# Attention scores as products 64 rows deep, with the queries as they were loaded

## The chip, the core and the metric

The kernel runs on one core of one Trainium2 chip. The time is what the device takes for one execution, in microseconds (us). The engines named are TensorE (PE, with its weight loads PEld), VectorE (DVE), ScalarE (ACT), GpSimd (POOL) and SyncE (SP), which here issues loads and stores.

## What is computed

Attention in eight heads over eight sequences of 576 tokens, then a mixture of eight experts with a capacity, greedily assigned. Cut to what matters:

```python
q, k, v: (8, 8, 576, 64) float32        # batch, head, token, depth
scores = q @ k.T / 8
rel = pos[:, None] - pos[None, :]
mask_plain = (rel >= 0) & (rel < 32)                    # heads 0 to 3
mask_dil = (rel >= 0) & (rel < 128) & (rel % 4 == 0)    # heads 4 to 7
attn = softmax(where(mask, scores, -1e9))
x = attn @ v                            # (4608, 512) after merging heads
logits = x @ w_gate                     # (4608, 8)
# the pairs (token, expert) in order of falling logit, each token to one expert, 576 tokens to each
for e in range(8):
    out[mask_e] = relu(x[mask_e] @ w1[e]) @ w2[e]
```

## The kernel before

The program has two parts, attention and the experts, with the router between them. In each part a small planner (`Schedule`, line 154) takes operations with an engine, an estimated cost, their dependencies, a due time and, for products, a pool of PSUM tiles; it runs through them in planned time and writes every engine's instructions down in the order that it finds. On the chip each engine then works through its own list in that order.

**Units.** Attention goes through 32 units, four a batch: two of plain heads, two of dilated ones, each for two heads (the two halves `a`). The depth is 64, so two heads stand above each other in the 128 partitions. A plain unit has 9 blocks of 64 queries against 96 keys; a dilated one, after sorting the tokens by residue, 12 blocks of 48 queries against 80 keys.

**Queries.** `load` (line 340) brings the queries of a batch into a staging tile `QS` and copies them from there into `QT` (lines 362 to 367), where each block has 2 x 64 columns (the dilated 2 x 48 of 128) and each head only its own half of the rows, with zeros in the other half, put there once by `zero` (line 311). A product over all 128 rows against these columns gives both heads' scores beside each other. The copies are spread over GpSimd, VectorE and ScalarE (`Q_ENG`). Queries, keys and values have two buffers, by the parity of the batch.

**One unit** (`build`, line 420):

- `scan` (line 482): bf16 products of the upper halves of the float32 words, 128 rows by 128 columns of queries against the block's keys; `most` (line 487) finds each row's masked maximum with VectorE; one product (line 436) turns the maxima, and a VectorE copy puts them into `R` (line 440).
- `scores` (line 495), in three groups of 3 (plain) or 4 (dilated) blocks: a bf16 selector product (line 501) adds mask and maximum for each block, then the float32 product of keys and queries (line 504) adds the scores. A float32 product stands in the trace as two records, each with a weight load. The weights are the block's keys (96 or 80 columns), and the queries are streamed.
- an exponential on ScalarE for each group (line 454), from PSUM into `E`.
- `values` (line 506): for each block and head a product with `V` into 64 partitions of a tile; `weigh` (line 514) divides by the sums.

**After the units** (`banks`, line 543): results are transposed (line 562) and kept in `xt` by ScalarE. After the last unit of a batch come the router's logits: four products whose weights are the padded gate weights `wgp`, one in each quarter of the columns, over 288 tokens (line 588), a copy into `L4` (line 596), a transpose for each 128 tokens (line 607), and a VectorE sum over the four quarters into `Lt` (line 613). `choose` then makes keys for the router, and `coarse` and `coarse_counts` (lines 707 and 712) count them into columns of the PSUM tile `pz`, chunk by chunk, with a low due time.

**PSUM** has eight banks: two for `scan`, two for `scores`, three (`PV`) shared by values, transposes and logits, and one, `pz`, for the router. Until the kernel is warm one of the three is used for idle products that keep the clock up.

SP's list holds the loads and stores in order; a load of keys waits for the scores of two batches before, since those read the same buffer.

Of the kernel before, what the change touches and what calls it, by code (L numbers as in the profile page):

```python
# [30 lines left out]
NK = 16  # L31
# [104 lines left out]
class Buf:  # L136
    def __init__(self, pool):
        self.pool, self.users, self.tile = pool, [], None
# [15 lines left out]
class Schedule:  # L154
# [18 lines left out]
    def place(self, x):  # L173

        best = None
        for i, h in enumerate(x.buf.pool.held):
            if h and any(u.end is None for u in h.users):
# [63 lines left out]
def attention(tc, ctx, C, load_const, T, xd, Lt, R):  # L241
# [8 lines left out]
    def ring(pool, shape, dtype, name, n):  # L250
# [7 lines left out]
    QS = [ring(pk, [128, 2, S] if x == 0 else [128, 8, SR], F32, f"qs{x}", 1) for x in range(2)]  # L258
# [6 lines left out]
    L4 = ring(pk, [128, 2 * S], F32, "L4", 1)  # L265
    PRE = ring(pk, [128, 256], BF, "pre", 2)
    wgp = pk.tile([128, 4, 32], F32, name="wgp")
# [4 lines left out]
    def qv(kind, s):  # L272
        t = QT[kind][s]
        if kind == 0:
            return t.rearrange("p (u c a i) -> p u c a i", u=2, c=NB, a=2)
        return t.rearrange("p (h c a i) -> p h c a i", h=8, c=3, a=2)
# [34 lines left out]
    def zero(kind, s, part, eng):  # L311

        jx = slice(part, part + 1) if kind == 0 else slice(4 * part, 4 * part + 4)
        t = qv(kind, s)[:, jx]
        e = nc.vector if eng == "DVE" else nc.gpsimd

        def fn():
            e.memset(t[64:, :, :, 0], 0.0)
            e.memset(t[:64, :, :, 1], 0.0)
            if kind == 1:  # L320
                for a in range(2):
                    e.memset(t[64 * a:64 * a + 64, :, :, a, QB[1]:], 0.0)

        ready["z", kind, s, part] = op(eng, 1200 if eng == "DVE" else 1000 if kind == 0 else 1700, fn)

# [14 lines left out]
    def load(b, kind, part=None):  # L340
# [7 lines left out]
        if not part:  # L348
            load.q = QS[kind].take()
            load.old = old("k", kind, s)  # L350
        qs, oldq, useq = load.q
        lq = sp(1, lambda: nc.sync.dma_start(qs[:, ix], q[b][:, ix]), oldq, nb, b)
        lk = sp(1, lambda: nc.sync.dma_start(KT[kind][s][:, ik], k[b][:, ik]), load.old, nb, b)
        dst = qv(kind, s)
        nq = QB[kind]
        oldd = old("q", kind, s) if not part else []
        for p in range(2) if part is None else (part,):
            cs = []
            for a in range(2):
                pr = slice(64 * a, 64 * a + 64)  # L360
                jx = slice(p, p + 1) if kind == 0 else slice(4 * p, 4 * p + 4)
                src = qs[pr, jx].rearrange("p u (c i) -> p u c i", i=nq)
                o = dst[pr, jx, :, a, :nq]
                eng = Q_ENG[kind][2 * p + a] if b else ("ACT", "DVE")[a]
                f = {"ACT": act, "DVE": nc.vector.tensor_copy, "POOL": nc.gpsimd.tensor_copy}[eng]
                cost = {"ACT": 670, "DVE": 370 if kind else 670, "POOL": 2050}[eng]
# [1042 lines left out]
```

## Time and profile before

| | us |
|---|---|
| median of 3 runs | 728.65 (728.17 to 731.08) |
| run of the profiled execution | 729.1 |
| its span | 727.3 |
| TensorE products, busy | 672.8 (93%) |
| weight loads, busy | 589.5 (81%) |
| VectorE, busy | 499.1 (69%) |
| ScalarE, busy | 280.5 (39%) |
| GpSimd, busy | 121.5 (17%) |

The page divides the span into 40 slices of 18.2 us; each digit is the busy share of a slice in tenths, PEclk the granted TensorE clock in tenths, and the last row what the DMA engines moved in GB/s.

```profile
PE   6979999999984799998799999999999999999994
PEclk9889999999995799999799999999999999999998
DMA  9999987874120620812612702621441474122001
GB/s 255 246 254 321 284 248 223 247 202 107 36 66 31 211 59 19 278 52 66 204 58 53 248 35 66 200 99 52 148 150 51 146 232 160 44 94 95 1 23 43
```

Attention takes the first twelve slices (to 212 us), the router's first search the thirteenth (to 240 us), and the rest is the experts. A record of a product lasts longer than the engine is held by it, since products are pipelined: what counts is the distance from one start to the next.

### The profile page before, as it was taken

Reading aid. Unit: us, or ns where it says so; the run is one execution under the profiler, and the core shown is the slowest. Engines: PE = TensorE matmul, PEld = TensorE weight load, DVE = VectorE, ACT = ScalarE, POOL = GpSimd, SP = SyncE. Lnnn points to the kernel's source line nnn. Section 1 sums busy time; section 2 is a strip of 40 time slices with the busy share of each in tenths; the row PEclk is TensorE's granted clock in tenths of the full one; section 3 lists DMA queues with packets and bytes.
Section 4 is the critical chain, followed back from the end, with each engine's and each line's share of the span. In section 5 each row is a group of like instructions: output and inputs, shape, how many; then the busy total and the mean of one; then the engine's idle time right before and its main releaser. Section 6 shows DMA issues by size and latency. Waiting matters only on the chain.

```text
span 727.3 us, 17284 instructions
## 1 busy us (share of the span) xinstructions
PE 672.8 (93%) x6554; PEld 589.5 (81%) x6555; DVE 499.1 (69%) x2109; ACT 280.5 (39%) x593; POOL 121.5 (17%) x180
## 2 busy tenths in 40 slices
PE   6979999999984799998799999999999999999994
PEld 4868899899964498797579979978978988988983
DVE  5546776878647798888769969968967973733300
ACT  2335545453430631542433623523533434434210
POOL 6111111000000300500310410321131041041011
PEclk9889999999995799999799999999999999999998
DMA  9999987874120620812612702621441474122001
GB/s 255 246 254 321 284 248 223 247 202 107 36 66 31 211 59 19 278 52 66 204 58 53 248 35 66 200 99 52 148 150 51 146 232 160 44 94 95 1 23 43
DMA packets 55067, 98.30 MB, mean 135 GB/s; under 512 B 5828, under 2 KB 27460, under 8 KB 54980
## 3 DMA queue, kind: packets, MB, share of 16 engines
q1 hardware_dynamic: 49096, 78.32, 36.6%
q0 software_dynamic: 5888, 18.88, 7.7%
q8 instruction: 51, 0.84, 0.5%
q14 instruction: 32, 0.26, 0.1%
HBM read 78.31 MB, written 18.87 MB: 134 GB/s over the span
## 4 chain that ended last, share of the span: by engine, by line
PE 56%; DVE 15%; issue 13%; DMA 11%; POOL 2%; ACT 1%; SPq 1%; POOLq 0%; DVEq 0%; ACTq 0%
PE py L1275 14%; PE ph L1233 13%; PE pS L504 7%; PE px L512 5%; DMA xg<-xd,idx 3%; DMA qs<-in_qd 3%; DMA qs<-in_qp 3%; PE px L562 2%; DVE hb L1253 2%; PE pS L501 2%; PE ptx L1196 2%; DVE G L734 2%; PE pm L484 2%; PE py L1278 2%; PE py L1280 2%
## 5 line engine op out<-in xcount | busy, mean ns | idle before, releaser
L1275 PE MATMUL py<-w2h,hb 128*128 128x512 f32 x512 | 172.6, 402 | 0.0
L1233 PE MATMUL ph<-xh,w1h 128*128 128x256 f32 (+1 forms) x512 | 138.7, 301 | 0.5 <-ACT xh L1078 0.5
L1233 PE MATMUL ph<-xl,w1h 128*128 128x256 f32 (+1 forms) x512 | 136.3, 297 | 0.0
L1233 PE MATMUL ph<-xh,w1l 128*128 128x256 f32 (+1 forms) x512 | 136.3, 297 | 0.0
L1275 PEld LDWEIGHTS py<-w2h,hb 128*128 128x128 f32 x512 | 97.3, 190 | 19.8
L1078 ACT ACTIVATE hb<-ph 128x256 fp32r<-128x256 f32 (+2 forms) x192 | 59.7, 346 | 117.5 <-PE ph L1233 117.0
L1275 PE MATMUL py<-w2l,hb 128*128 128x512 f32 x256 | 101.0, 394 | 1.0 <-DVE w2l L1079 1.0
L1233 PEld LDWEIGHTS ph<-xh,w1h 128*128 128x128 f32 x512 | 91.8, 189 | 1.2 <-ACT xh L1078 0.6
L1233 PEld LDWEIGHTS ph<-xl,w1h 128*128 128x128 f32 x512 | 91.5, 189 | 0.0
L1233 PEld LDWEIGHTS ph<-xh,w1l 128*128 128x128 f32 x512 | 91.5, 189 | 0.0
L504 PE MATMUL pS<-q,k 128*80 128x96 f32 (+1 forms) x672 | 84.5, 268 | 0.0
L1301 POOL DMA_INDIRECT out<-y,idx x40 | 41.5, 1038 | 223.4 <-ACT y L1078 157.4
L1253 DVE SCALAR_TENSOR_TENSOR hb<-ph,hb 128x256 fp32r<-128x256 f32 (+1 forms) x128 | 57.0, 452 | 24.6 <-ACT hb L1078 24.2
L454 ACT ACTIVATE E<-pS 96x384 f32<-96x384 f32 (+1 forms) x96 | 46.1, 486 | 67.3 <-PE pS L504 58.4
L504 PEld LDWEIGHTS pS<-q,k 128*80 128x80 f32 (+1 forms) x672 | 70.0, 161 | 0.0
L1078 ACT ACTIVATE y<-py 128x512 f32<-128x512 f32 (+1 forms) x40 | 23.9, 596 | 110.5 <-PE py L1275 98.5
L491 DVE CUSTOM_DVE_ANT_0 junkm<-pm,const 128x80 bf16<-128x80 f32 (+1 forms) x336 | 59.7, 243 | 8.9 <-PE pm L484 8.5
L1275 PEld LDWEIGHTS py<-w2l,hb 128*128 128x128 f32 x256 | 48.8, 191 | 10.2 <-DVE w2l L1079 1.5
L1079 DVE TENSOR_TENSOR w2l<-raw,w2h 128x512 fp32r<-128x512 f32 x64 | 42.1, 684 | 19.4 <-ACT w2h L1078 19.2
L1078 ACT ACTIVATE w1h<-raw 128x512 fp32r<-128x512 f32 x64 | 39.7, 630 | 35.8 <-DMA raw<-in_moe_w 35.3
L512 PE MATMUL px<-v,E 81*64 81x65 f32 (+1 forms) x1344 | 48.5, 227 | 4.3 <-DMA v<-in_vp 1.8
L1183 POOL DMA_INDIRECT xg<-xd,idx x40 | 43.3, 1082 | 45.0 <-issue 30.3
(160 smaller groups left out, 993.6 us busy)
## 6 DMA issues: line engine op xcount, KB each, us to landing
raw<-in_moe_w SPq DMA_DIRECT2D x128, 256.0 KB, 4.5
v<-in_vp SPq DMA_DIRECT2D x8, 780.0 KB, 9.9
v<-in_vd SPq DMA_DIRECT2D x8, 650.0 KB, 9.5
xd<-xs SPq DMA_DIRECT2D x16, 288.0 KB, 8.8
xd<-xs SPq DMA_DIRECT2D x32, 144.0 KB, 8.6
qs<-in_qp SPq DMA_DIRECT2D x7, 576.0 KB, 9.3
k<-in_kp SPq DMA_DIRECT2D x7, 576.0 KB, 4.0
k<-in_kd SPq DMA_DIRECT2D x7, 576.0 KB, 5.7
```

The costliest lines, as they stand in the source:

```text
L454: e = self.op("ACT", 380, lambda j=j, pS=pS: nc.scalar.activation(self.E[:self.nk, j * self.gs:j * self.gs + self.gs], pS.tile[:, :self.gs ...
L484: nc.tensor.matmul(pm[:, (c - c0) * self.nk:(c - c0 + 1) * self.nk], self.Qh[c], self.Kh[c], start=True, stop=True)
L491: nc.vector.tensor_tensor_reduce(out=jk[:, c - c0, :nk], in0=pm[:, (c - c0) * nk:(c - c0 + 1) * nk], in1=mm[:, min(1, (c if self.kind == 0 ...
L504: nc.tensor.matmul(pS[:nk, c - c0], self.Ks[c], self.Qm[c], start=False, stop=True, skip_group_check=True)
L512: nc.tensor.matmul(px[64 * a:64 * a + 64, c - c0], lh, self.V[c][a], start=True, stop=True)
L1078: act = lambda o, i, f=AF.Copy: nc.scalar.activation(o, i, f)
L1079: sub = lambda e, o, a, b: e.tensor_tensor(o, a, b, op=OP.subtract)
L1183: nc.gpsimd.indirect_dma_start(out=xg[:n], out_offset=None, in_=xd, in_offset=bass.IndirectOffsetOnAxis(ap=box[0][:n, m:m + 1], axis=0))
L1233: nc.tensor.matmul(o, a[:, d * 128:d * 128 + 128], b[:, d, c0:c1], start=((d, i) == pairs[0]), stop=((d, i) == pairs[-1]))
L1253: hl = op("DVE", 335 if j == 0 else 400, lambda: nc.vector.scalar_tensor_tensor(hb[:, CAP + c0:CAP + c1], o, 0.0, hb[:, c0:c1], op0=OP.max ...
L1275: nc.tensor.matmul(py, x, w, start=(f + i == 0), stop=(f == NF - 1 and i == 2))
L1301: s = nc.gpsimd.indirect_dma_start(out=out, out_offset=bass.IndirectOffsetOnAxis(ap=box[0][:n, m:m + 1], axis=0), in_=y[:n], in_offset=None)
```

## The change

Queries are loaded straight into `QT`; the staging tiles, the copies and the zeroed halves are gone. A block's scores are two products, one for each head, each over that head's 64 rows; the two heads' results lie in different banks of a PSUM tile that has two. The selector product is split in the same way, though it keeps its 73 or 76 rows. `scan` too has two products a block, from 64 rows into 64 partitions each. The exponential reads both banks and writes `E` in the order of before.

The logits have tokens in partitions: `xt` is the weight (128 tokens), and the gate weights are streamed (8 columns), four products a chunk of 128 tokens that add up in PSUM; a batch of 576 tokens has four whole chunks and a half one. Two VectorE copies bring them into `Lt`. The transposes of line 607 and the tile `L4` are gone.

PSUM: two banks for `scan`, two tiles of two banks for `scores` and now the transposes of line 562 too, and for values and logits one bank and `pz`. Since `pz` is in use until then, the router's coarse counts are all made after the last unit, from flags kept for all chunks; the flags are made as before. `Buf` can now ask for one certain tile of its pool.

The planner's costs change with it (in ns).

```diff
+C_S = 620
-Q_ENG = (("POOL", "POOL", "POOL", "ACT"), ("DVE", "DVE", "ACT", "ACT"))
...
-    QT = [[pk.tile([128, 2 * NB * 128] if x == 0 else [128, 8 * 3 * 128], F32, name=f"q{x}{s}") for s in range(2)]
+    QT = [[pk.tile([128, 2 * S] if x == 0 else [128, 8 * SR + 16], F32, name=f"q{x}{s}") for s in range(2)]
...
-    PM, PS, PV = (Pool([ps.tile([128, 512], F32, name=f"{n}{i}") for i in range(k)])
-                  for n, k in (("pm", 2), ("pS", 2), ("px", 3)))
+    PM = Pool([ps.tile([128, 512], F32, name=f"pm{i}") for i in range(2)])
+    PS = Pool([ps.tile([128, 2, 512], F32, name=f"pS{i}") for i in range(2)])
+    PV = Pool([ps.tile([128, 512], F32, name="px0"), R.pz])
...
+        n = (S, SR)[kind]
+        dst = QT[kind][s][:, :2 * S].rearrange("p (u n) -> p u n", n=n)
+        lq = sp(1, lambda: nc.sync.dma_start(dst[:, ix], q[b][:, ix]), load.old[0], nb, b)
+        lk = sp(1, lambda: nc.sync.dma_start(KT[kind][s][:, ik], k[b][:, ik]), load.old[1], nb, b)
         for p in range(2) if part is None else (part,):
...
+            ready["q", kind, b, p] = [lq, lk]
...
-            self.Qm = [Q[:, x, c, :, :nq] for x, c in L]
-            self.Ks = [K_[:, x, k0[c]:k0[c] + nk] for x, c in L]
+            two = [slice(0, 64), slice(64, 128)]
+            self.Qm = [[Q[p, x * nq0 + nq * c:x * nq0 + nq * c + nq] for p in two] for x, c in L]
+            self.Ks = [[K_[p, x, k0[c]:k0[c] + nk] for p in two] for x, c in L]
...
-                a = self.op("PE", 42 * (c1 - c0), lambda c0=c0, c1=c1, pm=pm: self.scan(c0, c1, pm.tile), qk, B_A, pm)
+                a = self.op("PE", 40 + 50 * (c1 - c0), lambda c0=c0, c1=c1, pm=pm: self.scan(c0, c1, pm.tile),
+                            [*qk, ready["pad"]] if kind else qk, B_A, pm)
...
-                d = self.op("DVE", (177 if kind == 0 else 162) * (c1 - c0),
+                d = self.op("DVE", (290 if kind == 0 else 270) * (c1 - c0),
...
-                c = self.op("PE", 850, lambda j=j, pS=pS: self.scores(j, pS.tile), [rc, *qk, ready["c", 1 + kind]], 0, pS)
+                c = self.op("PE", C_S, lambda j=j, pS=pS: self.scores(j, pS.tile), [rc, *qk, ready["c", 1 + kind]], 0, pS)
...
             for c in range(c0, c1):
-                nc.tensor.matmul(pm[:, (c - c0) * self.nk:(c - c0 + 1) * self.nk], self.Qh[c], self.Kh[c],
-                                 start=True, stop=True)
+                for a in range(2):
+                    nc.tensor.matmul(pm[64 * a:64 * a + 64, (c - c0) * nk:(c - c0 + 1) * nk], self.Qh[c][a], self.Kh[c][a],
+                                     start=True, stop=True)
...
+            o = lambda c, a: pS[:nk, a, (c - c0) * nq:(c - c0 + 1) * nq]
             for c in range(c0, c0 + gs):
+                for a in range(2):
+                    nc.tensor.matmul(o(c, a), ls[:64 + n, c], self.r[:64 + n, a * nq:a * nq + nq], start=(c == c0), stop=False,
+                                     skip_group_check=True)
             for c in range(c0, c0 + gs):
+                for a in range(2):
+                    nc.tensor.matmul(o(c, a), self.Ks[c][a], self.Qm[c][a], start=False, stop=True, skip_group_check=True)
...
+        def logits():
+            for c, p, n in h + parts:
+                o = pt.tile[p:p + n, NE * (c - c0):NE * (c - c0) + NE]
                 for g in range(4):
+                    t0 = 128 * c + p - b * S
+                    nc.tensor.matmul(o, xt_[b, g // 2][0][:, g % 2, t0:t0 + n], wg[:, g], start=(g == 0), stop=(g == 3))
```

More of the change, by code (lines that the diff above doesn't have):

```diff
@@ L136, with __init__ @@
 class Buf:
-    def __init__(self, pool):
-        self.pool, self.users, self.tile = pool, [], None
+    def __init__(self, pool, only=None):
+        self.pool, self.users, self.tile, self.only = pool, [], None, only
 class Ring:
@@ L176, in place @@
         for i, h in enumerate(x.buf.pool.held):
-            if h and any(u.end is None for u in h.users):
+            if h and any(u.end is None for u in h.users) or x.buf.only not in (None, i):
                 continue
@@ L309, in attention @@
     ready = {}
[L311 to L324, printed above, removed]
     def frame(kind):
@@ L348, in load @@
         if not part:
[L349 to L356, printed above, removed]
-        for p in range(2) if part is None else (part,):
[L358 to L366, printed above, removed]
-                c = op(eng, cost, lambda o=o, src=src, f=f: f(o, src), [lq, ready["z", kind, s, p], *oldd], -4 * b * P_U)
-                useq.append(c)
-                cs.append(c)
-            ready["q", kind, b, p] = [*cs, lk]
+            load.old = old("q", kind, s), old("k", kind, s)
+        n = (S, SR)[kind]
+        dst = QT[kind][s][:, :2 * S].rearrange("p (u n) -> p u n", n=n)
+        lq = sp(1, lambda: nc.sync.dma_start(dst[:, ix], q[b][:, ix]), load.old[0], nb, b)
+        lk = sp(1, lambda: nc.sync.dma_start(KT[kind][s][:, ik], k[b][:, ik]), load.old[1], nb, b)
+        for p in range(2) if part is None else (part,):
+            ready["q", kind, b, p] = [lq, lk]
     def load_values(b, kind):
@@ new lines, in banks, with settle @@
+        t = un.op("PE", 2000, logits, [*xt_[b], ready["w"]], B_K, pt)
+        for kk in range(2):
+            xt_[b, kk][2].append(t)
+        def settle():
+            for c, p, n in h:
+                nc.vector.tensor_copy(Lt[p:p + n, c], pt.tile[p:p + n, NE * (c - c0):NE * (c - c0) + NE])
+            ca = parts[0][0]
+            nc.vector.tensor_copy(Lt[:, ca:c1], pt.tile[:, NE * (ca - c0):NE * (c1 - c0)].rearrange("p (c e) -> p c e", e=NE))
+        x = un.op("DVE", 340, settle, [t], B_K)
@@ L631, in attention @@
-    fill, warm = PV.tiles[2], R.zero
-    PV.held[2] = Buf(PV)
+            f = op("DVE", 196, lambda c=c: R.coarse(c, PRE[:, c]), [x], late)
+            if c == 0:
+                counts.append([])
+            counts[0].append((c, f))
+        if b < B - 1:
+            return
+        hold = Buf(PV, 1)
+        hold.users.append(Op(-1, "PE", 0, None, (), 0, 0, 0, None))
+        prev = None
+        for c, f in counts[0]:
+            prev = op("PE", 60, lambda c=c: R.coarse_counts(c, PRE[:, c]), [f, ready["c", 3], prev, un.last], late,
+                      buf=None if prev else hold)
@@ L633, in attention @@
+    counts = []
+    fill, warm = PS.tiles[1][:, 0], R.zero
+    PS.held[1] = Buf(PS)
     keep_clock(nc, warm, fill, F0)
@@ L641, in idle, with pad @@
                 keep_clock(nc, warm, fill, int(max(0, gap - 400) / 430))
-    zero(0, 0, 0, "DVE")
-    zero(0, 0, 1, "POOL")
-    for kind, s in ((1, 0), (0, 1), (1, 1)):
-        for part in range(2):
-            zero(kind, s, part, "POOL")
-    op("DVE", 300, lambda: nc.vector.memset(R.pz[:, :256], 0.0), (), B_P)
+    def pad():
+        for s in range(2):
+            nc.gpsimd.memset(QT[1][s][:, 8 * SR:], 0.0)
+    ready["pad"] = op("POOL", 200, pad)
     for part in range(2):
@@ L812, in search_alone @@
             nc.vector.tensor_scalar(flag[:w, 1:], ps, float(CAP), None, op0=OP.is_ge, op1=OP.max, accum_out=flag[:w, :1])
+            if it == 2 and not last:
+                nc.vector.memset(self.pz[:, :256].rearrange("p (c k) -> p c k", k=32)[:, :, NK:], 0.0)
             nc.tensor.matmul(self.pa[:, :1 + NE], C[f"unit{it}"][:w], flag[:w], start=True, stop=True)
```

92 lines of the change are left out of this document (23 added, 69 removed).

## The prediction

> **What bounds the kernel now.** I read the stretches of 20 us first (columns: length; busy us and count of TensorE products, of its weight loads, of VectorE, ScalarE and GpSimd; granted clock; DMA share; GB/s), then TensorE's waits in the first 212 us.
>
> ```profile
> 0.00:20.00 20.00, 13.96 (x126) 10.23 (x127) 11.26 (x74) 5.71 (x10) 11.78 (x30) 0.91 0.91 261
> 20.00:40.00 20.00, 17.33 (x277) 16.05 (x274) 10.53 (x76) 5.54 (x11) 2.18 (x4) 0.91 1.05 241
> 40.00:60.00 20.00, 15.72 (x232) 14.34 (x233) 7.78 (x60) 9.05 (x17) 1.99 (x3) 0.83 1.01 273
> ...
> 120.00:140.00 20.00, 20.00 (x348) 17.95 (x347) 14.19 (x91) 9.44 (x18) 1.99 (x3) 1.00 0.69 214
> ...
> 180.00:200.00 20.00, 20.00 (x327) 18.32 (x327) 13.93 (x96) 8.58 (x17) 0.00 (x0) 1.00 0.14 32
> ```
> ```profile
> PE pm L484 <- DVE q L367: 6.0, 2, 5.3
> PE px L512 <- DMA v<-in_vp: 1.8, 1, 1.8
> PE px L512 <- DMA v<-in_vd: 1.6, 1, 1.6
> PE pm L436 <- DVE mx L491: 1.5, 2, 1.1
> ```
>
> Attention lasts until about 212 us of the span. Up to 60 us the DMA engines are full, TensorE now and then waits (the four largest waits: 10.9 us together), and its clock is granted at 0.91, 0.91 and 0.83, which is 7 us of full clock lost. From 100 us on the DMA share falls and TensorE has no pause: 20.00 of 20. A busy TensorE is a modelled figure, so I checked it in the timeline of its products (start, length with overlap, count):
>
> ```profile
> 98.65 0.33 PE L501 MATMUL pS<-R,const 73*96 73x128 bf16 x3
> 98.82 0.85 PE L504 MATMUL pS<-q,k 128*96 128x128 f32 x6
> 99.50 0.33 PE L501 MATMUL pS<-R,const 73*96 73x128 bf16 x3
> 99.67 0.85 PE L504 MATMUL pS<-q,k 128*96 128x128 f32 x6
> 100.36 0.33 PE L501 MATMUL pS<-R,const 73*96 73x128 bf16 x3
> 100.53 0.85 PE L504 MATMUL pS<-q,k 128*96 128x128 f32 x6
> 101.31 1.28 PE L512 MATMUL px<-v,E 97*64 97x65 f32 x36
> 102.51 0.22 PE L436 MATMUL pm<-const,mx 128*12 128x128 bf16 x1
> 102.66 0.87 PE L562 MATMUL px<-const,xs 128*128 128x128 f32 x6
> 103.37 0.38 PE L484 MATMUL pm<-k,q 128*128 128x96 bf16 x5
> 103.59 0.33 PE L501 MATMUL pS<-R,const 76*80 76x96 bf16 x4
> 103.77 0.85 PE L504 MATMUL pS<-q,k 128*80 128x96 f32 x8
> 104.45 0.34 PE L484 MATMUL pm<-k,q 128*128 128x96 bf16 x4
> 104.63 0.33 PE L501 MATMUL pS<-R,const 76*80 76x96 bf16 x4
> 104.80 0.85 PE L504 MATMUL pS<-q,k 128*80 128x96 f32 x8
> 105.49 0.38 PE L484 MATMUL pm<-k,q 128*128 128x96 bf16 x5
> ```
>
> Each group starts when the one before has been fed. So what a piece costs is the distance from its start to the next start, and the change is worth what it does to these distances. A float32 product stands there as two records (three blocks, x6), each with a weight load of its own.
>
> **Three prices from these rows.** *Scores, one group.* Plain head: selector 98.65 to 98.82, 0.17; products 0.68; 0.85 in all. Dilated: 0.18 + 0.68 = 0.86.
>
> *Changing how the array is divided.* The last record of line 504 before the values starts at 101.10, so the values should follow 0.11 later; they start at 101.31. Line 436 streams 128 columns, which takes line 501 0.055 (three in 0.17); the next piece starts 0.15 after it, at 102.66. Both are about 0.095 us more than the streaming: the array empties between products that fill all columns and those that use 64 or 12. Between lines 504, 501, 562 and 484, all undivided, nothing is lost.
>
> ```profile
> 101.10 0.27 PE L504 MATMUL pS<-q,k 128*96 128x128 f32 x1
> ```
>
> *Weight loads.* The loads' groups by shape, 80 to 208 us (rows*columns; busy us, mean ns):
>
> ```profile
> L504 PEld LDWEIGHTS pS<-q,k 128*80 128x80 f32 x283 | 25.4, 150 | 0.0
> L504 PEld LDWEIGHTS pS<-q,k 128*96 128x96 f32 x180 | 20.5, 163 | 0.0
> L512 PEld LDWEIGHTS px<-v,E 97*64 97x64 f32 x360 | 11.4, 137 | 1.5
> ...
> L501 PEld LDWEIGHTS <-const 73*96 73x96 bf16 x90 | 7.9, 123 | 0.9 <-issue 0.7
> ...
> L436 PEld LDWEIGHTS <-mx 128*12 128x12 bf16 x10 | 0.8, 84 | 1.0 <-DVE mx L491 0.3 <-issue 0.2
> ```
>
> From 64 to 96 float32 columns the load grows by 26 ns, 0.81 ns a column; the rest is latency that overlaps. So 96 columns hold the load path for 78 ns, 80 for 65, 128 for 104. Where a load is not hidden one sees it: the first load of a group starts at 100.47, the second at 100.56, and with 80 columns at 103.72 and 103.79.
>
> ```profile
> 100.47 0.16 PEld L504 LDWEIGHTS pS<-q,k 128*96 128x96 f32 x1
> 100.56 0.17 PEld L504 LDWEIGHTS pS<-q,k 128*96 128x96 f32 x1
> 103.72 0.15 PEld L504 LDWEIGHTS pS<-q,k 128*80 128x80 f32 x1
> 103.79 0.23 PEld L504 LDWEIGHTS pS<-q,k 128*80 128x80 f32 x2
> ```
>
> I take 0.083, 0.069 and 0.110 us, swap included. In bf16, (123 - 84)/84 = 0.46 ns a column: 0.045 for 96, 0.037 for 80. Today every score load hides behind a stream as long or longer (128 or 96 columns, 0.109 or 0.083 us a record). That is what the change undoes: it halves the streams (64 or 48 columns) and leaves the loads at 96 and 80.
>
> **The change, part by part.**
>
> *Products.* Each block's product becomes two, 64 rows deep, one for each half. No row shows halves split by rows. By columns it is shown: 36 records of line 512 in 101.31 to 102.51 are 0.033 each, though each streams 65 columns in two steps (0.055), so two run at a time, their loads too. I take the same here: three blocks x two passes = 6 pairs, each as long as its load: 6 x 0.083 + the last stream 0.054 = 0.55; dilated 8 x 0.069 + 0.04 = 0.59. Ends: streams alone, 6 x 0.056 and 8 x 0.043, both 0.34; no overlap, 12 x 0.083 = 1.00 and 16 x 0.069 = 1.10.
>
> *Selector.* Twice the records with half the columns: 6 x 0.045 = 0.27 and 8 x 0.037 = 0.30, against 0.17 and 0.18 if the load stayed hidden.
>
> *Array emptied on the way in.* The selector is 73 or 76 rows deep, so it can't stand in a half: whole array, then halves. I take 0.095 from the column case; ends 0 and 0.15 (the distance with the load behind it). The group: 0.27 + 0.095 + 0.55 = 0.915 against 0.85; dilated 0.30 + 0.095 + 0.59 = 0.985 against 0.86. Sum 0.19 x 48 = **+9 us**.
>
> The Trainium skill, "TensorEngine Tiling (Array Packing)", "Key Properties", says that a change of tiling mode drains TensorE, and it lists 64-row tiles as a mode of their own; by that the 0.095 holds for rows too, and the trace agrees for columns alone. Its "TensorE: Matmul & The Clock Gate", "LDWEIGHTS", has the load go by columns and not by rows, so that 64 rows would shorten none; no row here shows a 64-row load.
>
> *On the way out.* The last group of a unit is followed by its values, where the division changes today already (100.53). The other groups above (98.82, 99.67, 103.77, 104.80) are followed by a piece where today nothing changes and then something would. Two of three, 64 of 96, each 0.095 + a bf16 load of 0.045 that no stream hides = 0.14: **+9 us**.
>
> *Scan* (line 484): from 128x128 to two 64x64 quarters a block, 45 ns as before if they overlap; each scan changes the division, about one new change per scan beyond those counted: 64 x 0.12 = **+8 us**. Ends 0 and 64 x 0.35 = 22 (quarters one after the other).
>
> *Logits.* Line 588 took 1.11 (113.17 to 114.28, below), the transposes of line 607 0.11 each, 4.5 a batch: 1.6 together. Now tokens are the weights: 4 chunks x 4 x 2 loads of 128 columns, and 8 of 64: 32 x 0.110 + 8 x 0.055 = 3.96, and the half chunk of 64 tokens divides the columns, 0.24. +2.6 x 8 = **+21 us**. If the loads cost half: 2.2, +5 us.
>
> ```profile
> 113.17 1.18 PE L588 MATMUL px<-xt,wgp 128*32 128x288 f32 x16
> 114.28 0.62 PE L484 MATMUL pm<-k,q 128*128 128x80 bf16 x12
> ```
>
> *Removed: query copies and zeroing.* No byte of DMA goes: as many loads, into the query tile itself, in SP's same order; a query load now waits for the scores two batches back instead of a copy, and behind it on SP stands the key load, which waits for the same scores today. The copies are off the path after 60 us: GpSimd waited on TensorE, not the reverse.
>
> ```profile
> POOL q L367 <- PE pS L504: 58.8, 6, 18.2
> ```
>
> So nothing there. Early they bring what TensorE waits: of 10.9 us of waits and 7 us of lost clock I take **-12 us**, which a longer TensorE covers in any case; ends -18 and 0.
>
> *PSUM.* Score groups and 7 transposes a batch share two slots, each held some 1.5 us (0.9 TensorE, 0.49 the exponential below, and latencies): 19 x 1.5 / 2 = 14 us of a batch. A batch is four units, and the unit above lasts from 98.65 to 103.59, 5 us, before its logits. Cost nothing, hidden by TensorE's other pieces; at most +5.
>
> ```profile
> L454 ACT ACTIVATE E<-pS 96x384 f32<-96x384 f32 (+1 forms) x96 | 46.1, 486 | 67.3 <-PE pS L504 58.4
> ```
>
> *Counts* (line 712) move behind the last unit, where TensorE waits for VectorE: nothing, at most +2. The planner's new costs put the same pieces in another order; with TensorE never short of work I take nothing, ends -3 and +3. VectorE loses copies and is not the bound (14 of 20).
>
> Sum: 9 + 9 + 8 + 21 - 12 = **+35 us**. The profiled span is 727.3, its run 729.1, the median of three 728.65; I add to the median: **763**. Router and experts, from 212 us, are as before.
>
> **Rivals.** *A. Row halves don't empty the array.* No row excludes it. Then 9 + 9 of the drains go (96 x 0.095 and the way out): +17, **745**.
>
> *B. Faster: the loads don't bind.* If a load in a half holds the path only half as long, products take 0.34, the selector 0.17, and the array isn't emptied for rows: -0.31 x 96 = -30, scan +8, logits +5: -17, of which the first 45 of 212 us, full of DMA, give little: -15, **714**. It decides from loads of about 0.7 of their length, where the sum of A before the covered waits (28 to -17) crosses zero. Against it stand 0.09 and 0.07 in the four load rows. The Trainium skill, "TensorEngine Tiling (Array Packing)", "Theoretical Speedup", promises up to 2x at 64 rows, which is this case.
>
> *C. The halves don't overlap* (the change doesn't do what it says): products +0.45 and +0.51 a group, 48 x 0.96 = +46 on top: **809**.
>
> *D. B's loads, but the array is emptied:* -17 + 18, about **729**.
>
> **Numbers.** Forecast 0.47, A 0.16, B 0.22, C 0.06, D 0.09. B and a quarter of D come out faster by over 0.5% (about what a measurement of this kernel tells from no change): 0.24; within it 0.06, most of D; slower 0.70, the rest. The range 710 to 785 takes in B, D, A and the forecast with its ends (clock and waits, PSUM); C is left out. The slower cases alone span 740 to 785.
>
> **What would show it.** Right: score pairs 0.083 apart (plain) and 0.069 (dilated), a gap of some 0.1 at lines 501 to 504 and back, logits near 4 us a batch, attention ending near 247 us. Wrong: pairs 0.055 apart (B), no gap (A), single products 0.083 apart (C). If TensorE pauses on ScalarE or VectorE after 100 us, the PSUM step is wrong.

## The result, and the profile after

The changed kernel takes 869.04 us (median of 4 runs, 855.38 to 882.97) against 729.69 (4 runs): a ratio of **1.180, interval 1.166 to 1.193**. The forecast of 763 and its whole range, to 785, were far too low. The ratio is that of the two shorter runs (855.38 and 866.04, mean granted clock 0.837 and 0.822); the profiled execution is one of the two longer, with a run of 872.05, a span of 870.3 and a clock of 0.816.

First the page's slices of the changed kernel's span (40, each 21.8 us, in tenths; PEclk is the granted clock):

```profile
PE   6999999999999999749999799999999999999995
...
PEclk7556555559688575559999799999999999999998
```

TensorE is busy at nine tenths and more in nearly every slice, and its clock is granted in half through most of the first sixteen. The stretches of attention say it in numbers (columns as in the prediction: length; busy us and count of TensorE products, weight loads, VectorE, ScalarE, GpSimd; granted clock; DMA share; GB/s). The changed kernel:

```profile
0.00:60.00 60.00, 51.97 (x679) 44.63 (x684) 21.77 (x180) 10.06 (x19) 0.59 (x10) 0.60 0.99 251
60.00:200.00 140.00, 139.89 (x1683) 125.91 (x1679) 49.66 (x364) 29.54 (x56) 0.00 (x0) 0.54 0.41 120
200.00:219.00 19.00, 19.00 (x382) 17.30 (x379) 10.16 (x71) 5.59 (x11) 0.00 (x0) 1.00 0.53 131
219.00:345.00 126.00, 125.09 (x1781) 113.51 (x1780) 45.11 (x298) 32.39 (x63) 0.00 (x0) 0.68 0.29 83
```

The kernel before:

```profile
60.00:212.00 152.00, 149.37 (x2490) 134.44 (x2487) 110.78 (x738) 73.29 (x141) 9.98 (x15) 1.00 0.70 195
```

The third number from the end is the one to read: before, the clock is whole from 60 us on; after, it is 0.54 and 0.68 in stretches in which TensorE has no pause (139.89 of 140, 125.09 of 126). Nor does it wait for another engine there; from 100 to 345 us the table of TensorE's waits has one row, 0.9 us:

```profile
PE pS L468 <- ACT xt L269: 0.9, 2, 0.4
```

The last batch's logits are the last large piece of attention (40 records from 348.73, 7.95 us at half clock). Behind them and the router's counts comes the first product of the router's search, of line 745 now and of line 788 before. In the timelines (start, length, count), after:

```profile
359.57 0.25 PE L745 MATMUL py<-flagc,const 128*128 128x1 bf16 x2 [0.27 <-DVE junkc L742]
```

Before:

```profile
217.05 0.25 PE L788 MATMUL py<-flagc,const 128*128 128x1 bf16 x2 [0.27 <-DVE junkc L785]
```

What follows took 727.3 - 217.1 = 510 before and 870.3 - 359.6 = 511 now, so **all of the loss, some 142 us, is in attention**.

The changed kernel has its full clock for twenty microseconds at a time, and there its pieces can be timed as the prediction did, from start to start. In the changed kernel line 468 is the selector, 472 the scores, 449 the scan, 398 the turn-product, 559 the logits. Its timeline of TensorE at full clock:

```profile
204.35 0.57 PE L449 MATMUL pm<-k,q 64*64 64x96 bf16 x18
204.88 0.44 PE L468 MATMUL pS<-R,const 73*96 73x64 bf16 x6
205.25 0.72 PE L472 MATMUL pS<-q,k 64*96 64x64 f32 x12
205.90 0.46 PE L468 MATMUL pS<-R,const 73*96 73x64 bf16 x6
206.28 0.72 PE L472 MATMUL pS<-q,k 64*96 64x64 f32 x12
206.94 0.22 PE L398 MATMUL pm<-const,mx 128*9 128x128 bf16 x1
...
209.64 0.48 PE L468 MATMUL pS<-R,const 76*80 76x48 bf16 x8
210.05 0.78 PE L472 MATMUL pS<-q,k 64*80 64x48 f32 x16
210.76 0.48 PE L468 MATMUL pS<-R,const 76*80 76x48 bf16 x8
```

A plain group is 1.02 and 1.04 (204.88, 205.90, 206.94), a dilated one 1.12; the scan of nine blocks is 0.53, where 45 ns a block before make 0.40. And a batch's 40 logits records at full clock:

```profile
215.37 4.30 PE L559 MATMUL pz<-wg,xt 128*64 128x8 f32 x40
```

The same group at half clock:

```profile
106.59 0.66 PE L468 MATMUL pS<-R,const 73*96 73x64 bf16 x6
107.18 1.23 PE L472 MATMUL pS<-q,k 64*96 64x64 f32 x12
108.34 0.27 PE L398 MATMUL pm<-const,mx 128*12 128x128 bf16 x1
```

That is 1.75, 1.7 times as long. So the loss can be added up. The added work at full clock is what the prediction summed: 9 + 9 + 8 + 21 = 47. The clock lost in attention, from the four rows, is 0.40 x 60 + 0.46 x 140 + 0.32 x 126 = 129 us of full clock, and 7 more from 345 us to the end at half clock. A piece that takes 1.7 at half clock and 1 at full loses 0.7/1.7 = 0.41 of its time, not half, so I estimate that 136 x 0.41/0.5 = 112 could be had back. The kernel before lost 7 us of full clock, or 6 in the same way. 47 + 112 - 6 = 153, against some 142 measured. The rest may be half clock that full DMA queues hid in the first 60 us, and early waits that went; the two largest, 6.0 and 1.8 us before, are now these:

```profile
PE pm L449 <- DMA k<-in_kp: 3.4, 2, 2.8
PE pS L468 <- ACT E L416: 2.3, 5, 0.6
```

**The work forecast is there, and twice as much again is clock.**

### The profile page after: what moved, and what is told of

It is laid out like the page before. It is cut to its first block, busy times and chain, and to the rows that moved or that the text cites. A ratio compares the mean times of both kernels' runs of the same rounds, so it can differ in the third digit from the quotient of the medians.

```text
span 870.3 us, 20086 instructions
## 1 busy us (share of the span) xinstructions
PE 824.2 (95%) x8056; PEld 728.3 (84%) x8060; DVE 485.4 (56%) x2074; ACT 266.5 (31%) x567; POOL 95.2 (11%) x138
## 3 DMA queue, kind: packets, MB, share of 16 engines
q8 instruction: 63, 1.03, 0.5%
## 4 chain that ended last, share of the span: by engine, by line
PE 71%; DVE 11%; issue 10%; DMA 3%; POOL 2%; ACT 1%; SPq 1%; POOLq 0%; DVEq 0%
PE py L1234 13%; PE ph L1192 12%; PE pS L472 11%; PE pS L468 6%; PE pS L530 4%; PE px L480 4%; PE px L559 4%; PE pz L480 4%; PE pm L449 3%; PE pz L559 2%; DMA xg<-xd,idx 2%; DVE hb L1212 2%; PE ptx L1155 2%; DVE G L691 1%; PE py L1237 1%
## 5 line engine op out<-in xcount | busy, mean ns | idle before, releaser
L472 PE MATMUL pS<-q,k 64*80 64x48 f32 (+1 forms) x1344 | 103.2, 312 | 0.0
L472 PEld LDWEIGHTS pS<-q,k 64*80 64x80 f32 (+1 forms) x1344 | 88.2, 219 | 4.8
L976 POOL TENSOR_TENSOR rx<-oa,const 128x360 bf16<-128x360 bf16 x8 | 7.5, 936 | 497.3 <-DVE oa L971 497.3
L468 PE MATMUL pS<-R,const 76*80 76x48 bf16 (+1 forms) x672 | 58.4, 235 | 3.5 <-ACT E L416 2.3
L468 PEld LDWEIGHTS <-const 76*80 76x80 bf16 (+1 forms) x672 | 49.6, 160 | 11.0 <-issue 3.4
L1234 PEld LDWEIGHTS py<-w2l,hb 128*128 128x128 f32 x256 | 48.8, 191 | 10.2 <-DVE w2l L1038 1.5
L269 ACT ACTIVATE xt<-pS 128x288 f32<-128x288 f32 (+1 forms) x56 | 32.2, 604 | 69.1 <-PE pS L530 67.5
```

Source lines behind the costliest of these rows:

```text
L468: nc.tensor.matmul(o(c, a), ls[:64 + n, c], self.r[:64 + n, a * nq:a * nq + nq], start=(c == c0), stop=False, skip_group_check=True)
L472: nc.tensor.matmul(o(c, a), self.Ks[c][a], self.Qm[c][a], start=False, stop=True, skip_group_check=True)
L1234: nc.tensor.matmul(py, x, w, start=(f + i == 0), stop=(f == NF - 1 and i == 2))
```

## The experiments

The question was why a TensorE that never pauses keeps half its clock. Three features of the changed work were suspects: that it streams little for the weights it loads, that its products are 64 rows deep, and that it divides the array anew all the time. The expectations number the theories as they stood when each was written. Where a kernel computes no attention, its expectation says so; its rows have one column less (no ScalarE).

### m1_clock: which products lose the clock?

Nine kinds of products, each after 60 products of 512 columns that set the clock to full.

- whole array, 96 loaded, 128 streamed
- 64-row pairs, 96 loaded, 64 streamed
- 64-row pairs, 96 loaded, 256 streamed
- whole array, 96 loaded, 64 streamed
- 128 loaded, 8 streamed (logits)
- plain groups (selector, 6 pairs)
- scan in quarters; scan undivided
- 64 rows alone, 256 streamed

> Leaves out the whole computation: the output is zeros, and TensorE runs nine stretches of one kind of product each, every stretch after 60 idle products of 512 columns (some 13 us at full clock) that bring the clock up. Question: which kind of product loses the granted clock. Theory 1 (the gate counts the time in which columns are streamed): the stretches whose load is longer than their stream fall to 0.5 a few us after they begin, whether rows are divided or not: pairs 64 rows deep with 96-column loads and 64 streamed (share of streaming 0.65), the same undivided, the 128-column loads with 8 streamed (0.06), and the group of selector and pairs (about 0.47). Those that stream all the time stay at 1.0: 96 loaded and 128 streamed, pairs with 256 streamed, the scan whole, 64 rows alone with 256 streamed. Theory 2 (the gate counts how much of the array works): everything 64 rows deep loses it, the pairs with 256 streamed less than 64 rows alone; undivided products keep it, load-bound or not. Theory 3 (emptying the array): only the group of selector and pairs loses it. At full clock I expect, per record: 109 ns (96 loaded, 128 streamed); 83 ns a pair divided by rows; 216 ns a pair with 256 streamed; 83 ns undivided with 64 streamed; 110 ns with 8 streamed; 1.0 us a group; 45 ns a pair of the divided scan, 44 ns whole; 216 ns for 64 rows alone.

Its stretches: the 64-row pairs, the logits' kind up to the loss and behind it, the groups, 64 rows alone.

```profile
59.90:90.60 30.70, 30.70 (x721) 30.63 (x721) 0.00 (x0) 0.00 (x0) 1.00 0.01 3
...
190.60:193.10 2.50, 2.50 (x25) 2.50 (x24) 0.00 (x0) 0.00 (x0) 1.00 0.00 0
193.20:247.00 53.80, 53.80 (x254) 53.80 (x254) 0.00 (x0) 0.00 (x0) 0.50 0.00 1
262.40:293.70 31.30, 31.19 (x541) 27.99 (x541) 0.00 (x0) 0.00 (x0) 1.00 0.01 2
391.60:419.00 27.40, 27.40 (x128) 20.36 (x128) 0.00 (x0) 0.00 (x0) 1.00 0.00 1
```

Only the logits' kind loses the clock, after 2.6 us, while TensorE is busy in every one of them (53.80 of 53.80). A pair is 30.70 / 360.5 = 85 ns: both halves overlap and the load binds, as forecast. Neither the 64 rows nor the division loses the clock by itself, for 30 us at least. That explains the logits, 4 us eight times, and not some 260 of the first 345 us at half clock: what was missing was why the clock doesn't come back.

### m2_regain: which products bring it back?

Nine stretches of the same sort, each now begun at half clock, behind 60 products of the logits' kind; between the two parts of a group stood 0, 2, 4 or 8 products of zeros (192 columns).

> Leaves out the whole computation: the output is zeros. Before each of nine stretches stand 60 products with 128-column loads and 8 streamed columns, the kind that alone lost the clock in the run before (2.7 us after it began), so that every stretch begins at 0.5. Question: which mix of products gets the clock back. Theory 4 (the gate has two thresholds: little streaming loses the clock, and only much streaming regains it): the group of selector and pairs, whose streams fill 0.47 of its time and which kept the clock in the run before, does not regain it in its 30 rounds (60 us at half clock); with 2, 4 and 8 added undivided streams of 192 columns (0.54, 0.59 and 0.68 of the time) it regains at some number of them; the group of the kernel before (selector and products undivided, streams back to back) regains within 3.4 to 7 us, as do pairs with 256 streamed. Pairs alone and undivided products with 64 streamed (both 0.65 streaming) come out alike if division plays no part, and only the undivided ones regain if the share of the array counts; 64 rows alone with 256 streamed then do not regain either. Theory 5 (no second threshold; the kernel after loses the clock again and again by something else): every stretch regains it within 7 us.

Up to 587 us the clock column of this trace reads 1.00, though the products there take twice their time (128-column loads 214 ns apart, 25.74 us for 120, where m4_dilated has 107 at full clock, 6.30 us for 59): the trace's record of the clock begins there. So the first stretches are read by the distances alone. Never regained: the plain group (with 2, 4 and 8 fillers too), 64-row pairs with 64 streamed, the whole array with 96 loaded and 64 streamed, 64 rows alone. Regained: the group of before, and 64-row pairs with 256 streamed, the latter here:

```profile
641.00:645.40 4.40, 4.40 (x23) 3.01 (x24) 0.00 (x0) 0.00 (x0) 0.50 0.00 0
645.60:665.00 19.40, 19.40 (x182) 14.70 (x180) 0.00 (x0) 0.00 (x0) 1.00 0.00 1
```

The timeline shows the two that decide (start, length, count):

```profile
501.66 57.66 PE L192 MATMUL p<-q,k 128*96 128x64 f32 x359
...
696.89 61.42 PE L192 MATMUL p<-q,k 64*96 64x256 f32 x146
```

160 ns a record through 57 us, where m1_clock took 85, with all 128 rows: so it is not the 64 rows alone. And some 430 ns a record through 61 us (140 of its own and a few neighbours), where m1_clock took 214, although it streams without a pause: so it is not streaming alone either. Both count: the share of the time in which columns are streamed, times the share of the 128 rows that they go through. **The limit for getting the clock back is much higher than that for losing it.** The same two kinds kept a full clock in m1_clock.

### e1_after_old_logits and e2_after_old_logits_burst: the changed kernel with the logits of before

```diff
-                    nc.tensor.matmul(o, xt_[b, g // 2][0][:, g % 2, t0:t0 + n], wg[:, g], start=(g == 0), stop=(g == 3))
+        (logits, L4, wgp and the seven transposes of the kernel before)
```

e2 adds 20 products of 512 columns in the second group of the second unit, after the start's waits:

```diff
+                if u == 1 and g == 1:
+                    pb = Buf(PS)
+                    pb.users.append(self.op("PE", 20 * 216, lambda pb=pb: keep_clock(nc, R.zero, pb.tile[:, 0], 20), [d], B_V, pb))
```

> The changed kernel with the logits of before (padded gate weights, quarters of the columns, transposes of line 607); all else as changed. Theory 4 (two thresholds: the 128-column loads with 8 streamed columns lose the clock, and the groups of 64-row pairs keep the clock they have but do not regain a lost one): the eight losses at the logits are gone, those by waits in the first 45 us stay and are not regained for some tens of us. At full clock 763 - 21 = 742; with 10 to 30 us for the half clock at the start 750 to 775, granted clock near 1.0 from 100 us to the end of attention. Rival (64-row products or the emptied array lose the clock by themselves): 869 - 21, about 845, clock at 0.5 through most of attention.

> As e1, with 20 idle products of 512 columns after the values of the second unit. Theory 4: they bring the clock back early (20 x 0.216 to 0.43 = 4 to 9 us), and then nothing loses it: 742 + 4 to 9, about 749, less than e1. Rival: the clock falls again right after: e1 + 7.

e1: 771.86 against 728.47, ratio 1.056 (1.045 to 1.068). Its stretches:

```profile
9.00:53.00 44.00, 41.02 (x560) 37.11 (x562) 18.11 (x146) 6.64 (x14) 0.00 (x0) 0.50 1.04 257
53.00:251.00 198.00, 190.48 (x3883) 161.23 (x3881) 112.84 (x773) 71.62 (x140) 0.00 (x0) 1.00 0.57 162
```

Without the new logits the clock, once back at 53 us, stays for the rest of attention, as expected, and the time lies within the 750 to 775 expected (the rival's was 845). By the ratio +41 us is what is left, although all the divided work of the changed kernel is in it: 9 + 9 + 8 of added work and 44 x 0.41 = 18 of lost clock, less the 6 of before, make 38. e2 took 780.52 (773.35 to 809.34) and no ratio could be given: the burst brought the clock back at 32.7 us, a pause of 2.7 us took it away again at 46.3, and a third loss came at 135.1, beside a pause of 0.65. A burst there is no cure.

### e4_before_new_logits: the kernel before with the new logits alone

> The kernel before with the new logits alone. Full clock: 32 x 0.110 + 8 x 0.055 + 0.24 - 1.6 = +2.6 a batch, +21: 750. Theory 4: the clock may fall at each batch's logits and is regained in 3.4 to 7 us by the undivided groups: up to 4 us a batch more, 750 to 782, about 765; granted clock 0.8 or more in each 20 us of 60 to 200 us. Rival: the clock stays at 1.0 and it is 750.

778.93, ratio 1.064 (1.056 to 1.072): **+50 us, where the added work is 21**. Its stretches from 1 us after the start of one batch's logits (75.40):

```profile
76.50:86.50 10.00, 10.00 (x57) 9.98 (x58) 4.71 (x32) 1.93 (x4) 1.35 (x2) 0.50 0.53 159
87.00:107.00 20.00, 20.00 (x318) 18.78 (x316) 11.43 (x78) 10.08 (x19) 0.66 (x1) 1.00 0.90 264
```

The clock falls 1 us into the logits, they go on at half, and it is back after 7 to 10 us. An undivided group takes 1.66 us at half clock (m2_regain, from 584.34 to 586.00) and 0.85 at full, so it loses 0.49 of its time: 8 x 8.5 x 0.49 = 33, against the 29 that the added work leaves open. In this kernel the mix of undivided work gives the clock back each time; in the changed one the same logits cost it for tens of microseconds.

### e3_after_bursts and e7_after_burst_at_once: bursts behind the logits

The changed kernel with e2's burst and 16 more such products after every batch's logits; in e7 these alone, at so high a rank that the planner puts them right behind the logits.

```diff
+        pb = Buf(PS)
+        pb.users.append(un.op("PE", 16 * 216, lambda pb=pb: keep_clock(nc, R.zero, pb.tile[:, 0], 16), [t], B_K + 40000, pb))
         x = un.op("DVE", 340, settle, [t], B_K)
```

> The changed kernel, logits and all, with 16 idle products of 512 columns after each batch's logits and 20 after the second unit: work added, nothing taken away. Theory 4: 763 at full clock, + 9 x 4 to 5 for the bursts + some 4 at half clock during the logits: about 808, so adding 32 us and more of products makes it some 60 us faster. Rival: 869 + 9 x 6, about 920.

> The changed kernel with 16 idle products of 512 columns right behind each batch's logits (in e3 the planner had put them 12 to 28 us later). Theory 4: the clock falls near the end of the logits and is back 3 to 7 us later, so each batch pays 4 to 7 us for the burst and 2 for the fall: 763 + 8 x 7 + 15 to 20 for the start = about 835, between e6 and the change. Rival: about 900.

e3 gave 866.73, ratio 1.173 (1.163 to 1.184), neither 808 nor 920. The planner put six of its eight bursts 7 to 22 us behind the end of the logits; a batch's logits (186.4), a burst (202.2), and up to the next logits (218.6):

```profile
186.40:191.20 4.80, 4.80 (x47) 4.74 (x46) 1.82 (x16) 0.54 (x2) 0.00 (x0) 1.00 0.97 309
191.40:202.20 10.80, 10.50 (x121) 9.12 (x122) 4.42 (x34) 3.40 (x7) 0.00 (x0) 0.50 0.33 94
202.20:204.80 2.60, 2.57 (x7) 0.91 (x7) 0.78 (x3) 0.00 (x0) 0.00 (x0) 0.50 0.00 0
205.00:218.60 13.60, 13.60 (x279) 11.35 (x276) 5.95 (x46) 4.11 (x8) 0.00 (x0) 1.00 0.46 141
```

This is the cleanest picture of the two limits in the kernel itself: logits take the clock, the divided work runs at half until a burst, seven of its products bring the clock back, and the same divided work then keeps it until the next logits. It does 121 records in 10.8 us at half clock and 279 in 13.6 at full (not quite the same mix). The half clock fell from 258 of the first 345 us to 184, worth 74 x 0.41 = 30 us; yet nothing was gained, since eight bursts of 16 and one of 20 are 148 products of some 0.216, 32 us, and more at half clock. e7 gave 855.36, ratio 1.174 (1.164 to 1.184), where 835 was expected. Its bursts do what they should:

```profile
200.40:207.10 6.70, 6.47 (x27) 5.04 (x28) 2.17 (x12) 0.00 (x0) 0.00 (x0) 0.50 0.02 6
207.30:237.80 30.50, 29.81 (x564) 25.68 (x563) 15.09 (x116) 9.09 (x18) 0.00 (x0) 1.00 0.63 179
```

But the clock also fell at 74.0 and 121.8, with no logits near: in a run of dilated groups, next to pauses of 1.9 and 0.9 us.

### e6_after_filled_logits: products of zeros inside the logits

Two after every second logits product, to raise what is streamed:

```diff
+                    for _ in range(2 * (g % 2)):
+                        nc.tensor.matmul(pt.tile[:, 64:], R.zero[:, :128], R.zero[:, 64:], start=False, stop=False,
```

> The changed kernel with two zero products of 448 streamed columns after every second pair of logits records, added to unused columns of the logits' own bank: 20 a batch, 8 x 20 x 0.187 = 30 us of work added and nothing taken away. Streams then fill half of the logits' time, above the 0.35 to 0.47 between which the clock is lost. Theory 4: no loss at the logits; 763 + 30 + some 15 to 20 for the half clock of the first 50 us (as in e1) = about 810, clock at 1.0 from some 60 us to the end of attention. Rival (the clock is lost by the 64-row products): 869 + 30, about 900.

852.35 (826.22 to 896.49), too scattered for a ratio, and not the 810 expected. Its stretches:

```profile
76.00:215.80 139.80, 139.00 (x1400) 117.12 (x1400) 38.57 (x277) 22.86 (x44) 0.00 (x0) 0.50 0.34 99
216.00:307.90 91.90, 91.21 (x1671) 79.41 (x1671) 45.48 (x328) 26.97 (x53) 0.00 (x0) 1.00 0.47 127
```

Filled logits cost the clock nothing: it lasted 92 us over three of them (233, 265 and 293). But it was lost at 75.8, again among dilated groups and at a pause of 2.15 us, and then stayed away for 140 us. That such small early events make the runs scatter is likely and not shown: only the longest run has a trace. The mean granted clocks of the four, 0.92 for 826.22, 0.88 for 851.50 and 853.20, 0.83 for 896.49, do go with their times.

### m3_thresholds and m4_dilated: where are the limits?

m3_thresholds: groups with 8 or 4 logits records added to each, four groups with 36, 128 columns loaded with 16, 32, 64 streamed, from full clock; seven kinds from half clock. m4_dilated: dilated and plain groups, 128 loaded with 48 to 60 streamed, dilated pairs alone, from full clock; 96 loaded with 68, 72, 76 streamed, from half clock.

> Leaves out the whole computation: the output is zeros. First six stretches that begin at full clock, after 60 idle products: the changed group with 8 records of logits behind each (streams 0.27 of the time), with 4 behind each (0.35), four groups and then 36 records (4 us of logits after 4 us of groups); 128-column loads with 16, 32 and 64 columns streamed (0.12, 0.25, 0.5). Then seven stretches that begin at 0.5: whole products with 96 columns loaded and 80 or 96 streamed (0.8 and 0.96), pairs 64 rows deep with 80, 96 and 128 streamed (0.8, 0.96, 1.0), whole products of 96 rows with 128 streamed (1.0, three quarters of the rows), and of 128 rows by 64 columns with 128 streamed (1.0, half of the columns). Theory 4 with one measure (share of time in which columns are streamed, times the share of rows used): losing lies between 0.06 and 0.47, regaining between 0.68 and 1.0. So the four groups with 4 us of logits lose it, the stretch with 16 streamed loses it, the one with 64 keeps it; 96 rows with 128 streamed (0.75) and pairs with 80 (0.8) do not regain if the limit is high, pairs with 128 do. Rival to the measure (only the time counts, and 64 rows alone failed for another reason): 96 rows with 128 streamed regain. That a narrow array (64 columns) regains would say that columns do not count.

> Leaves out the whole computation: the output is zeros. Each of the first seven stretches begins at full clock. In e6 and e7 the clock also fell in runs of dilated groups without logits. Their streams fill 8 x 0.020 + 8 x 0.040 = 0.48 of 1.12 us, 0.43; the plain groups' 0.48 of 1.04, 0.46. If losing lies between: 30 dilated groups lose the clock in some 3 to 10 us, 40 plain groups keep it, and of 128-column loads with 48, 52, 56 and 60 columns streamed (0.36, 0.39, 0.42, 0.45) the first three lose it; dilated pairs alone (0.040 of 0.069: 0.58) keep it. Rival (logits and waits alone lose it): the dilated groups keep it. Then three stretches that begin at 0.5, whole products with 96 loaded and 68, 72, 76 streamed (0.68, 0.72, 0.76 of 0.083): with one measure, the limit of regaining lies between 0.68 and 0.75, so 76 regains and 68 does not.

m3_thresholds, group with 4 logits records (behind its loss, which came after 6 us), 64 streamed (kept), 96 loaded and 80 streamed (regained):

```profile
105.00:146.00 41.00, 41.00 (x346) 38.17 (x345) 0.00 (x0) 0.00 (x0) 0.50 0.00 1
...
471.40:504.00 32.60, 32.60 (x295) 32.60 (x293) 0.00 (x0) 0.00 (x0) 1.00 0.01 2
...
531.70:554.00 22.30, 22.30 (x265) 22.30 (x264) 0.00 (x0) 0.00 (x0) 1.00 0.01 1
```

m4_dilated, dilated groups up to the loss and behind it, 48 streamed (behind its loss), 52 streamed, 68 from half clock:

```profile
15.90:21.70 5.80, 5.80 (x128) 5.37 (x127) 0.00 (x0) 0.00 (x0) 1.00 1.05 401
21.80:68.90 47.10, 46.82 (x596) 43.37 (x595) 0.00 (x0) 0.00 (x0) 0.50 0.22 83
...
144.80:195.00 50.20, 50.20 (x237) 50.20 (x237) 0.00 (x0) 0.00 (x0) 0.50 0.00 1
210.70:243.90 33.20, 33.20 (x300) 33.20 (x298) 0.00 (x0) 0.00 (x0) 1.00 0.01 1
...
397.60:445.00 47.40, 47.40 (x298) 47.40 (x298) 0.00 (x0) 0.00 (x0) 0.50 0.00 1
```

Each kind gets one number: the time that its columns stream (0.85 ns a float32 column, from 0.109 for 128 in the prediction; half that in bf16), over its time at full clock, times the rows used of 128. For the plain group: six pairs of 64 columns, 0.327, and six selectors, 0.163 x 73/128 = 0.093, over 1.03: 0.41.

| kind | number | from full clock | from half clock |
|---|---|---|---|
| 128 loaded, 8 streamed (logits) | 0.06 | lost | |
| group + 8, + 4 logits records | 0.25, 0.31 | lost | |
| 128 loaded, 48 streamed | 0.38 | lost | |
| **dilated group** | 0.38 | lost in 5.9 us | |
| 128 loaded, 52 streamed | 0.40 | kept | |
| **plain group** | 0.41 | kept | not regained |
| 64 rows alone, 256 streamed | 0.5 | kept | not regained |
| plain group, 8 fillers | 0.64 | | not regained |
| 96 loaded, 64 streamed, pairs or whole | 0.64 | kept | not regained |
| 96 loaded, 68 streamed | 0.69 | | not regained |
| 96 loaded, 72 streamed | 0.73 | | regained in 4.6 us |
| 96 rows deep, 128 streamed | 0.75 | | regained |
| group of before | 0.88 | | regained in 3 us |

The kinds not in the table fall on the same sides: lost with 16 and 32 streamed (0.12, 0.25) and in four groups with 36 logits records (0.24); kept with 56, 60 and 64 streamed (0.43, 0.46, 0.49) and in dilated pairs alone (0.57); regained with 80 and 96 streamed whole and in pairs of 80 to 128 (0.8 and more). One number orders all of them: **below 0.38 to 0.40 the clock is lost, and it comes back only above 0.69 to 0.73.** The number of columns used doesn't count: 64 of 128 columns, 128 rows deep with 128 streamed, regained. Several expectations put single limits elsewhere and missed: that 96 rows, or 80 streamed, wouldn't regain, that 52 and 56 streamed would lose.

The changed kernel's own groups, 0.41 and 0.38, thus stand on the lower limit and far under the upper one. The gate itself is not in the trace; the number is an account that fits these kinds. The kernels' own traces can test it. In each of them every stretch of full or half clock between two changes lasts a multiple of 3.41 us (51.2, 10.2, 126.3 and 20.5 us at first in the changed kernel), so the clock is set window by window. For each window of attention I estimated the number from its records: columns times 0.85 ns (half in bf16, twice at half clock), times rows of 128, with values, of which two run side by side, counted half, and the old logits, four side by side, a quarter.

| windows of attention | changed kernel | all ten kernels that compute it |
|---|---|---|
| clock lost behind it | 6, 0.06 to 0.38 | 54, up to 0.39 |
| full clock kept | 17, 0.39 to 0.60 | 429, from 0.36 (one 0.30) |
| half clock kept | 73, 0.06 to 0.75 | 269, up to 0.77 |
| clock regained behind it | 5, 0.76 to 0.86 | 56, from 0.69 |

The same two limits, within 0.04, hold in the kernel itself. So the early waits, the logits, and windows with little beside dilated groups take the clock. The groups don't give it back, but the transposes do (line 530, whole products that stream 128 columns) where they happen to gather in one window: all five returns of the changed kernel stand behind a run of them, here the one at 233.4.

```profile
228.59 1.54 PE L530 MATMUL pS<-const,xs 128*128 128x128 f32 x6
...
231.00 2.38 PE L530 MATMUL pS<-const,xs 128*128 128x128 f32 x9
```

No run tried to place them so. The group of before is over the upper limit, 0.88, and its three early losses lasted 3.4, 3.4 and 6.8 us.

### e5_before_split_scan and e8_before_logits_and_scan: the scan

The kernel before with the scan in quarters, and with the new logits as well.

```diff
-                nc.tensor.matmul(pm[:, (c - c0) * self.nk:(c - c0 + 1) * self.nk], self.Qh[c], self.Kh[c],
-                                 start=True, stop=True)
+                for a in range(2):
+                    p = slice(64 * a, 64 * a + 64)
+                    nc.tensor.matmul(pm[p, (c - c0) * self.nk:(c - c0 + 1) * self.nk], self.Qh[c][p, p], self.Kh[c][p],
+                                     start=True, stop=True)
```

> The kernel before with the scan alone in two 64x64 quarters a block, from the padded queries; the planner's costs as before. My step: 64 scans x 0.12 = +8 us (735 to 738), from the emptied array at each scan's ends; if the clock suffers too (less streaming at the edge of the limit in the first 60 us) up to +20. Rival: the quarters run one after the other, +22 (750).

> The kernel before with the new logits and the divided scan: everything that TensorE does differently except the 64-row scores and their selector. If the parts add: 779 (e4) + 7 (e5) = 786, and the 64-row scores then cost 869 - 786 = 83 in the change, of which my steps explain 18 at full clock; the rest is that they don't regain a lost clock. If the divided scan also delays regaining: up to 800.

e5: 735.70 (10 runs) against 728.68, ratio 1.0092 (1.0063 to 1.0121): +6.7 us, against 8 forecast and 22 if the quarters ran one after the other. e8: 778.85 against 732.82, ratio 1.067 (1.059 to 1.075), about e4's 1.064: on top of the logits the scan costs less than these intervals can tell (some 6 us either way). The parts don't add: by the ratios the logits alone cost 6.4%, all else without them 5.6%, both together 18.0%.

No version tried beats the kernel before.

## The prediction, step by step

**Failed: the granted clock.** The prediction knew it only as 7 us of loss at the start that a longer TensorE would cover, inside the -12, and made every sum at full clock. It came to some +106 (112 less the 6 of before), more than twice the added work. The prediction read a clock of 1.00 from 100 us on as a property of a TensorE that doesn't pause; the kernel before had it because its products stream 128 columns over 128 rows. No rival had this in it, so the range couldn't hold it. The rows of before could have raised the doubt: the clock was at 0.83 from 40 to 60 us with TensorE busy for 15.72 of 20 and waiting in the rest, so the clock does follow what TensorE does, and the change halves both the streams and the rows of a product and keeps its loads. Where the limits lie no row of before shows.

The Trainium skill, "TensorE: Matmul & The Clock Gate", "What's actually happening", has the clock halved after an idle window of about 3.4 us and given back after a busy one. The windows agree (every stretch is a multiple of 3.41 us), and so does the way back, 2.6 to 4.6 us in the stretches shown. The loss doesn't: 53.80 of 53.80 busy in m1_clock, with the clock at 0.50. The measurement decides: time in which weights are loaded and little is streamed doesn't keep the clock, though the profile counts it as busy.

**Right: the groups.** 1.02 to 1.04 and 1.12, where 0.915 + 0.14 and 0.985 + 0.14 were forecast. The selector takes 0.37 until the products start (0.27 + 0.095 forecast), 0.41 in the dilated group (0.395). That fits an array that empties when its rows are divided, on the way in and out, loads that bind, and halves that overlap (a pair 85 ns in m1_clock); rivals A, B, C and D fall. The rule of the Trainium skill, "TensorEngine Tiling (Array Packing)", "Key Properties", that changing the tiling mode drains TensorE fits the 0.10 for rows too. B's price was reckoned a little low: its own 0.34 and 0.17 make -0.34 a group, not -0.31, which puts it some 3 us lower; nothing hangs on it.

**Right: the logits' work** (4.30 for 40 records; 3.96 + 0.24 forecast), and its place, but not its price: +50 alone, since it takes the clock. **Right: the scan**, +6.7 for 8.

**Right: PSUM, counts, order.** 0.9 us of waits from 100 us on. **Right in part: the copies.** The early waits shrank, as the two rows above show; what the -12 held of the clock had the wrong sign.

## What to carry to other kernels

Before cutting products to fewer rows or shorter streams, work out for each few microseconds (here windows of 3.41) what share of TensorE's time streams columns, times the rows used; below about 0.4 the clock falls to half though TensorE is busy throughout, and between 0.4 and 0.7 a lost clock doesn't return until some window is above 0.7. A stage in that band runs well in a test that begins at full clock, so test it from half clock too, and time the whole kernel with each part alone and all together, since such losses don't add. Look at the granted clock before the busy share: busy says that TensorE has work, not how fast it does it.

## What the runs showed that was not expected

- Two limits, 0.38 to 0.40 and 0.69 to 0.73, on streaming share times row share, with TensorE busy all the time; rows count, columns don't.
- 64 rows alone, streaming without a pause, never bring the clock back (61 us at half).
- The clock changes only at multiples of 3.41 us; transposes that gather in one such window bring it back.
- The loss is quick: 2.6 us with 8 columns streamed, 5.9 with dilated groups. So is the way back, seven products of 512 columns in 2.6 us.
- Half the clock makes a divided group 1.7 times as long, not twice, though an undivided one (1.66 for 0.85) and 128-column loads (214 ns for 107) take about twice; which part of the divided group doesn't go by the clock no run separates.
